# Three PSUM banks for the expert units and three for the attention, instead of two and four

## The chip, the cores and the metric

The kernel runs on one core of one Trainium2 chip. The metric is the device time of one execution in microseconds (us); lower is better. The core has five engines with a queue of instructions each: TensorE (PE, matrix products, with PEld for its weight loads), VectorE (DVE), ScalarE (ACT), GpSimd (POOL) and SyncE (SP, which only issues transfers). Products of TensorE land in PSUM, a small memory of eight banks; here a bank holds 128 partitions by 512 float32 numbers. VectorE and ScalarE read the banks.

## The reference

Causal attention by blocks of 64 over 8 batches, 8 heads, 576 positions and a head size of 64, whose result, put back as 4608 rows of 512, goes through one gated layer with 2048 hidden features:

```python
scores = scale * np.matmul(q, k.transpose(0, 1, 3, 2))
scores = np.where(block_i >= block_j, scores, -1e9)
scores = scores - np.max(scores, axis=-1, keepdims=True)
attn = np.exp(scores)
attn = attn / (np.sum(attn, axis=-1, keepdims=True) + 1e-09)
x = np.matmul(attn, v)          # -> 4608 x 512
h = x @ w_in                    # 512 -> 2048
sp = np.maximum(h, 0.0) + np.log1p(np.exp(-np.abs(h)))
g = h * erf(sp)
return g @ w_out                # 2048 -> 512
```

## The kernel before

**The layer is cut into 144 units.** A unit is 256 rows of `x` by 256 hidden features: 18 blocks of rows times 8 blocks of features. `moe_unit` (L173) makes one. Its *up* part is 24 products of 256 columns (L185: two halves of the features, four slices of the 512 inputs, three terms, since `x` and the weights are kept as pairs of float16 numbers, a high and a low part) and fills one PSUM bank, `h`. `gate` (L145) then computes the gating function from that bank: ScalarE at L154 to L156, VectorE at L157 to L160, ScalarE again at L161 for the high part `gh`, and GpSimd at L162 for the low part `gl`. The bank `h` is read twice, by the first instruction (L154) and by the last of VectorE's (L160), so it is held from the first of the 24 products until L160 has ended. The *down* part is 12 products of 512 columns (L194) from `gh` and `gl` into two banks `o`, which collect over several units. Down parts run three units behind the up parts (`LAG = 3`, L221).

**The attention is cut into 64 heads.** For a head, `maxes` (L387) computes the scores once in five pieces (L394), whose row maxima VectorE takes (L397), and turns the maxima around (L424, ScalarE's copy L426, a transfer at L427). `probs` (L431) computes the scores a second time, transposed, in six pieces of two products each (L440, L441), of which ScalarE takes the exponentials (L445). `pv` (L464) multiplies them with `v` for two heads at a time (L489) and sums them (L512); ScalarE empties both (L492, L514, L515). `normalise` (L541) divides (L550, L551, L564, L569, VectorE's L571) and writes the rows of `x` to memory. Every piece of all this takes one PSUM bank from `bank` (L304), which the named reader empties.

**The eight banks.** `ps_o` has two (for `o`), `ps_h` two (for `h`) and `ps_a` four (for the attention). `bank` takes from `ps_a`, except in the first part of the run, before any rows of `x` are ready (`loaded` is empty): there the units need no bank yet, and of eight calls one goes to `ps_o` and two to `ps_h` (one bank of `ps_o` is held there by products that only keep TensorE busy, L645). When the attention is through, `ps_a` is closed and `ps_h2` takes two of its banks (L695); from there on units take turns between `ps_h` and `ps_h2` (L177).

**The order.** The loop at L648 goes over the heads and merges, at each, the steps of `maxes` two heads ahead, of `probs` for this head, of `pv` and `normalise` for earlier ones, of the weights' conversion (heads 1 to 22: L115 to L121, L141, L142) and of the units (`moe1`, L262: 12 steps at each of the first 20 heads, then 28; a unit is 12 steps). That order is a priority. The framework's scheduler puts the instructions of each engine into their final order when the program is built: it goes by the priority and by when operands and banks come free in its own estimate of the times. A tile gets its bank there as well. On the chip every engine works through its queue in that fixed order, and an instruction whose bank has not been emptied by its former reader holds up everything behind it on its engine.

So the run has four parts: the start, in which only attention runs (its first unit begins at 164.9 us); a part in which units, attention and the conversion of the weights run together; a long middle with units and attention; and an end with units alone.

Of the kernel before, what the change touches and what calls it, by code (L numbers as in the profile page):

```python
# [17 lines left out]
PSUM = bass.MemoryType.PSUM  # L18
# [14 lines left out]
def tile_attention_moe(ctx: ExitStack, tc: tile.TileContext, qk, v, w, maskrows, sels, out):  # L33
# [23 lines left out]
    xpool = ctx.enter_context(tc.tile_pool(name="xpool", bufs=2))  # L57
    mpool = ctx.enter_context(tc.tile_pool(name="mpool", bufs=3))
    ps_o = ctx.enter_context(tc.tile_pool(name="ps_o", bufs=2, space=PSUM))
    ps_h = ctx.enter_context(tc.tile_pool(name="ps_h", bufs=2, space=PSUM))  # L60

    ident = cpool.tile([P, P], F32, name="ident")
    make_identity(nc, ident)
# [59 lines left out]
    def scale_w(g, bank):  # L123

        rs = cpool.tile([P, 2], F32, name=f"wrs{g}")
        nc.vector.tensor_reduce(out=rs, in_=wss[g], axis=AX.X, op=ALU.add)
        pt = bank(f"wt{g}")
        nc.tensor.matmul(pt[:, :2], lhsT=ones, rhs=rs, start=True, stop=True)
        e = cpool.tile([P, 2], F32, name=f"we{g}")
        nc.vector.tensor_copy(e, pt[:, :2])  # L130
        nc.vector.tensor_scalar(out=i32(e), in0=i32(e), scalar1=23, scalar2=None, op0=ALU.logical_shift_right)
        nc.vector.tensor_scalar(out=i32(e), in0=i32(e), scalar1=131, scalar2=None, op0=ALU.add)
        nc.vector.tensor_scalar(out=i32(e), in0=i32(e), scalar1=1, scalar2=None, op0=ALU.logical_shift_right)
        powers(wsb[g][:, 0:2], wsb[g][:, 2:4], e, 15)
# [152 lines left out]
            todo.pop(0)()  # L287

    with tc.tile_pool(name="apool", bufs=2) as apool, tc.tile_pool(name="spool", bufs=1) as spool, \
            tc.tile_pool(name="ps_a", bufs=4, space=PSUM) as ps_a:  # L290
        pstage = [spool.tile([P, n], F32, name=f"p32_{i}") for i, n in enumerate(PN)]
        rss = [spool.tile([P, SH], F32, name=f"rs{i}") for i in range(3)]
        mxs = [spool.tile([P, 7], F32, name=f"mx{i}") for i in range(2)]
# [10 lines left out]
        def bank(name):  # L304

            turn.append(0)
            k = len(turn) % 8 if not loaded else 0
            if k in (2, 5):
                return ps_h.tile([P, 512], F32, tag="h", name=name)
            if k in (3,):  # L310
                return ps_o.tile([P, 512], F32, tag="o", name=name)
            return ps_a.tile([P, 512], F32, tag="a", name=name)
# [13 lines left out]
        def scale_v(b, qd, v32, vt):  # L326

            nm = f"{b}_{qd}"
            vm = apool.tile([P, 1], F32, tag="vm", name=f"vm{nm}")
            nc.vector.tensor_reduce(out=vm, in_=v32, axis=AX.XY, op=ALU.max, apply_absolute_value=True)  # L330
            pt = bank(f"vt{nm}")
            nc.tensor.transpose(out=pt[:1, :P], in_=vm, identity=ident)
            if qd == 0:
                nc.vector.tensor_reduce(out=top_v[b], in_=pt[:1, :P], axis=AX.X, op=ALU.max)
                if b < B32:
                    return
            vs = apool.tile([1, 2], F32, tag="vs", name=f"vs{nm}")
            vs_[b, qd] = vs
            e = apool.tile([1, 2], F32, tag="ve", name=f"ve{nm}")
            if qd:  # L340
                nc.vector.tensor_reduce(out=e[:, :1], in_=pt[:1, :P], axis=AX.X, op=ALU.max)
                nc.vector.tensor_tensor(out=e[:, :1], in0=e[:, :1], in1=top_v[b], op=ALU.max)
            nc.vector.tensor_scalar(out=i32(e[:, :1]), in0=i32(e[:, :1] if qd else top_v[b]), scalar1=23, scalar2=None, op0=ALU.logical_shift_right)
            nc.vector.tensor_scalar(out=i32(e[:, :1]), in0=i32(e[:, :1]), scalar1=77, scalar2=197, op0=ALU.max, op1=ALU.min)
            powers(vs[:, 0:1], vs[:, 1:2], e[:, :1], 10)
# [390 lines left out]
```

## Time and profile before

| | us |
|---|---|
| median of three runs | 1290.05 |
| the three runs | 1290.46, 1290.05, 1287.4 |
| the profiled execution | 1288.4 |
| its span, first to last instruction | 1286.6 |
| DVE busy in the span | 895.8 (70%) |
| ACT busy | 780.5 (61%) |
| POOL busy | 523.6 (41%) |
| mean granted clock of TensorE | 0.975 of full speed |

The profile is of one execution; its time stands 1.65 us under the median of the runs. "Busy" is the time in which an engine has an instruction in work. Matrix products overlap, and the ends of their records are modelled, so a TensorE that is always busy is not one at its peak; but time in which it is not busy is lost to it. Where the profile names a releaser ("DVE m_r L160") it is the instruction whose end was the last thing that the waiting one needed, with its line in the code.

### The profile page before, as it was taken

How to read it: one execution, taken by the hardware profiler on the slowest of the kernel's cores; microseconds unless marked ns; L12 is line 12 of the kernel's file. 1: busy time of each engine (PE TensorE's matmuls, PEld its weight loads, DVE VectorE, ACT ScalarE, POOL GpSimd, SP SyncE). 2: the span in 40 equal slices, each digit the busy share in tenths (PEclk: the TensorE clock that was granted, in tenths of full speed). 3: DMA queues.
4: the chain of work that ended last, by engine and by line, in shares of the span. 5: the costliest groups of instructions: out<-in, count | busy, mean ns of one | idle time of the engine just before them, and what ended most of it. 6: DMA issues, size and time to landing. Idle time of an engine off the chain costs nothing.

```text
span 1286.6 us, 23640 instructions
## 1 busy us (share of the span) xinstructions
PE 1200.5 (93%) x9108; PEld 810.2 (63%) x9108; DVE 895.8 (70%) x1583; ACT 780.5 (61%) x1555; POOL 523.6 (41%) x488
## 2 busy tenths in 40 slices
PE   1899999989999999999999999999999999999997
PEld 0455566556666666767667666766667667666664
DVE  3853689887567878688777778795777765555554
ACT  2453567667556666766666756666666775555553
POOL 4444435553435453545445344544445331321221
PEclk9887889989999999999999999999999999999999
DMA  9794566862454554453545444554444221221111
GB/s 250 210 218 97 125 170 172 229 148 67 109 122 121 135 133 110 105 143 114 110 114 124 111 109 128 131 122 100 115 112 113 63 69 52 82 66 50 53 63 50
DMA packets 95808, 151.74 MB, mean 118 GB/s; under 512 B 7804, under 2 KB 44988, under 8 KB 95696
## 3 DMA queue, kind: packets, MB, share of 16 engines
q1 hardware_dynamic: 69840, 93.34, 24.4%
q0 software_dynamic: 25216, 56.73, 21.5%
q8 instruction: 72, 1.18, 0.4%
q14 instruction: 40, 0.33, 0.1%
q10 hardware_dynamic: 640, 0.17, 0.1%
HBM read 121.73 MB, written 28.31 MB: 117 GB/s over the span
## 4 chain that ended last, share of the span: by engine, by line
PE 49%; DVE 26%; ACT 14%; DMA 5%; issue 4%; POOL 1%; SPq 0%; DVEq 0%; POOLq 0%; ACTq 0%
PE m_h L185 14%; PE o L194 14%; DVE m_r L158 5%; DVE m_r L157 5%; PE u L489 4%; DVE m_r L159 4%; DVE m_r L160 3%; PE t L440 3%; ACT m_r L155 3%; ACT m_r L154 3%; PE s L394 3%; ACT m_r L156 3%; PE t L441 3%; DVE mx L397 2%; PE us L512 2%
## 5 line engine op out<-in xcount | busy, mean ns | idle before, releaser
L185 PE MATMUL m_h<-xh,w 128*128 128x256 f16 x2304 | 476.9, 276 | 12.8 <-DVE m_r L160 12.5
L185 PEld LDWEIGHTS <-w 128*128 128x128 f16 x3456 | 326.7, 99 | 146.6 <-issue 24.1
L194 PE MATMUL o<-w,m_gh 128*128 128x512 f16 x1152 | 337.0, 382 | 10.5 <-DVE pt L235 6.4
L162 POOL TENSOR_TENSOR m_gl<-m_r,m_gh 128x512 f16<-128x512 f32 x144 | 174.3, 1211 | 403.6 <-ACT m_gh L161 362.8
L185 PE MATMUL m_h<-xl,w 128*128 128x256 f16 x1152 | 316.6, 275 | 0.0
L397 DVE TENSOR_REDUCE mx<-s 64x1 f32<-64x288 f32 (+4 forms) x384 | 174.8, 470 | 110.8 <-PE s L394 109.8
L157 DVE SCALAR_TENSOR_TENSOR m_r<-m_r 128x512 f32<-128x512 f32 x144 | 115.6, 803 | 171.1 <-ACT m_r L156 168.9
L445 ACT ACTIVATE p<-t 128x288 f32<-128x288 f32 (+4 forms) x384 | 146.0, 385 | 108.7 <-PE t L441 102.7
L194 PE MATMUL o<-w,m_gl 128*128 128x512 f16 x576 | 206.0, 384 | 0.3 <-POOL m_gl L162 0.3
L161 ACT CAST m_gh<-m_r 128x512 f16<-128x512 f32 x144 | 88.8, 617 | 192.0 <-DVE m_r L160 187.9
L440 PE MATMUL t<-qk 69*128 69x288 f32 (+4 forms) x384 | 168.0, 438 | 13.1 <-DMA qk<-mt 7.5
L394 PE MATMUL s<-qk 68*64 68x288 f32 (+3 forms) x384 | 150.9, 424 | 27.4 <-DVE mx L397 14.9
L382 POOL TENSOR_TENSOR qk<-st,qk 64x576 fp32r<-64x576 f32 x64 | 95.9, 1498 | 149.4 <-DMA qk<-qk 136.2
L154 ACT ACTIVATE m_r<-m_h,c,bs 128x512 f32<-128x512 f32 (+3 forms) x192 | 124.1, 666 | 45.1 <-PE m_h L185 43.0
L194 PEld LDWEIGHTS <-m_gh 128*128 128x128 f16 x1152 | 98.5, 98 | 67.2 <-issue 19.7
L158 DVE SCALAR_TENSOR_TENSOR m_r<-m_r,m_r 128x512 f32<-128x512 f32 x144 | 120.6, 837 | 2.8
L441 PE MATMUL t<-qk 128*128 128x288 f32 (+4 forms) x384 | 120.1, 313 | 0.0
L159 DVE SCALAR_TENSOR_TENSOR m_r<-m_r 128x512 f32<-128x512 f32 x144 | 115.7, 803 | 2.9
L383 POOL TENSOR_TENSOR qk<-st,qk 64x576 fp32r<-64x576 f32 x64 | 103.1, 1611 | 30.0 <-DMA qk<-qk 27.1
L457 DVE TENSOR_TENSOR p<-p,p 128x832 f16<-128x832 f32 x80 | 82.6, 1033 | 36.3 <-ACT p L456 36.2
L156 ACT ACTIVATE m_r<-m_r,c 128x512 f32<-128x512 f32 x144 | 103.7, 720 | 2.9 <-ACT m_r L155 0.8
L155 ACT ACTIVATE m_r<-m_r,c 128x512 f32<-128x512 f32 x144 | 103.8, 721 | 1.7
(98 smaller groups left out, 1484.9 us busy)
## 6 DMA issues: line engine op xcount, KB each, us to landing
qk<-qk POOLq DMA_DIRECT2D x64, 432.0 KB, 5.0
st<-qk SPq DMA_DIRECT2D x64, 288.0 KB
qk<-qk POOLq DMA_DIRECT2D x64, 288.0 KB, 5.2
raw<-w SPq DMA_DIRECT2D x32, 512.0 KB
v<-v SPq DMA_DIRECT2D x16, 640.0 KB
x_d<-xs POOLq DMA_DIRECT2D x32, 288.0 KB, 3.5
xh<-x_d SPq DMA_DIRECT2D x36, 256.0 KB
xl<-x_d SPq DMA_DIRECT2D x36, 256.0 KB
```

The lines of the kernel that those rows point to most:

```text
L154: nc.scalar.activation(r0s[:, :, lo:hi], h[:, :, lo:hi], AF.Tanh, bias=const(p1), scale=bss[b][g][:, 0:1])
L157: nc.vector.scalar_tensor_tensor(out=r0, in0=r0, scalar=c3, in1=r0, op0=ALU.add, op1=ALU.mult)
L158: nc.vector.scalar_tensor_tensor(out=r0, in0=r1, scalar=c4, in1=r0, op0=ALU.add, op1=ALU.mult)
L159: nc.vector.scalar_tensor_tensor(out=r0, in0=r0, scalar=c5, in1=r0, op0=ALU.add, op1=ALU.mult)
L162: nc.gpsimd.tensor_tensor(out=gl, in0=r0, in1=gh, op=ALU.subtract)
L185: nc.tensor.matmul(h[:, k, :], lhsT=wf[:, a, sl], rhs=x[:, cc, :], start=cc == 0 and i == 0, stop=cc == NCC - 1 and i == 2)
L194: nc.tensor.matmul(o[c], lhsT=a[:, sl], rhs=wf[:, b_, :], start=u == u0 and k == 0 and not lo and b_ == 2, stop=u == u1 - 1 and k == nu - ...
L394: nc.tensor.matmul(dst[:r, :w_], lhsT=qh[:K, i * P : i * P + r], rhs=kh[:K, k0 : k0 + w_], start=True, stop=True)
L397: nc.vector.tensor_reduce(out=mx[:r, col : col + 1], in_=src, axis=AX.X, op=ALU.max, negate=True)
L440: nc.tensor.matmul(s[:kk, :w_], lhsT=kh[:K, ks], rhs=qh[:K, q0 : q0 + w_], start=True, stop=False)
L441: nc.tensor.matmul(s[:kk, :w_], lhsT=klh[:, ks], rhs=qhl[:, q0 : q0 + w_], start=False, stop=True)
L445: nc.scalar.activation(p32s[part][:kk, c : c + w_ - skip], s[:kk, skip:w_], AF.Exp, scale=SCALE)
```

## The change

`ps_h` gets a third bank and `ps_a` loses its fourth. In the first part of the run, of eight calls of `bank` three now go to `ps_h` instead of two, and four instead of five to `ps_a`. All eight banks stay in use, and no instruction is added or taken away.

```diff
-    ps_h = ctx.enter_context(tc.tile_pool(name="ps_h", bufs=2, space=PSUM))
+    ps_h = ctx.enter_context(tc.tile_pool(name="ps_h", bufs=3, space=PSUM))
...
-            tc.tile_pool(name="ps_a", bufs=4, space=PSUM) as ps_a:
+            tc.tile_pool(name="ps_a", bufs=3, space=PSUM) as ps_a:
...
             k = len(turn) % 8 if not loaded else 0
-            if k in (2, 5):
+            if k in (2, 5, 7):
                 return ps_h.tile([P, 512], F32, tag="h", name=name)
             if k in (3,):
                 return ps_o.tile([P, 512], F32, tag="o", name=name)
             return ps_a.tile([P, 512], F32, tag="a", name=name)
```

## The prediction, made before the changed kernel was run

> **What bounds the kernel now.** I read the page's first two parts, then the busy time in the four parts of the run, then the waits of TensorE in each part, then single stretches of the timeline. The page first: the share of each engine, and in 40 slices the busy tenths of PE and its granted clock.
>
> ```profile
> PE 1200.5 (93%) x9108; PEld 810.2 (63%) x9108; DVE 895.8 (70%) x1583; ACT 780.5 (61%) x1555; POOL 523.6 (41%) x488
> ...
> PE   1899999989999999999999999999999999999997
> ...
> PEclk9887889989999999999999999999999999999999
> ```
>
> PE is the engine that is nearly always at work. By the parts of the run (window, its length, then busy time and count for PE, PEld, DVE, ACT and POOL, granted clock, DMA share, GB/s):
>
> ```profile
> 0.00:165.00 165.00, 125.87 (x692) 68.84 (x693) 92.23 (x203) 69.73 (x174) 72.43 (x90) 0.88 0.75 182
> 165.00:300.00 135.00, 122.42 (x906) 82.51 (x906) 120.04 (x226) 92.00 (x211) 66.20 (x57) 0.94 0.67 170
> 300.00:1075.00 775.00, 756.17 (x6154) 529.74 (x6153) 571.91 (x997) 509.91 (x1000) 338.81 (x302) 1.00 0.45 111
> 1075.00:1287.00 212.00, 196.09 (x1361) 129.14 (x1359) 111.58 (x161) 108.90 (x171) 46.17 (x40) 0.99 0.18 58
> ```
>
> In the middle (300 to 1075 us) PE rests 775.0 - 756.2 = 18.8 us, 2.4%; DVE is busy 74% of it and ACT 66%. There PE's queue sets the time: each us that PE waits less or more comes off or goes onto the run. From 165 to 300 us DVE is busy 120.0 of 135 us, 89%, and PE 122.4: both near the limit. Before 165 us the DMA share is 0.75 and PE rests 39 us; after 1075 us PE rests 16 us.
>
> What does PE wait for? First the `h` banks, whose release is L160. Lines from the views of L160 (who waited for it in the whole run: us, times) and of L185 in the middle (idle of PE and PEld ahead of L185 until L160 ended):
>
> ```profile
>   PE m_h L185: 12.5, 19
>   PEld L185: 7.0, 10
> ...
> L185 PE MATMUL m_h<-xh,w x1560: 269/273/437, 300.2 to 1074.4; 128*128 128x256 f16 x195
> ...
>   DVE m_r L160: 15.6, 22
> ```
>
> A unit has 16 of the products counted here, so 97 units start in the middle, one in 8 us. The whole run has 19.5 us of waits of PE and its weight loads for an `h` bank, 15.6 of them in the middle, in 22 waits of 0.71 us each; the same view of the last part has 3.4 us:
>
> ```profile
>   DVE m_r L160: 3.4, 5
> ```
>
> Then the banks of the attention, whose readers are L397, L445 and others: the two largest such waits of PE from 165 to 300 us, and the largest two of L394 and L440 in the middle.
>
> ```profile
> PE s L394 <- DVE mx L397: 3.2, 2, 2.4
> PE t L440 <- DVE mx L397: 2.6, 2, 1.8
> ...
> PE s L394 <- DVE mx L397: 0.6, 1, 0.6
> PE t L440 <- DVE mx L397: 0.5, 1, 0.5
> ```
>
> With four banks the middle loses about 1 us to them. The profile says: `h` is the short pool, `ps_a` is not. The question is what `ps_a` loses with its fourth bank.
>
> **The change, part by part. (1) The third `h` bank.** One unit start of the kind that waits, on the timeline (start, duration, engine, line; in brackets the idle time and what ended it):
>
> ```profile
> 494.54 0.67 DVE L160 SCALAR_TENSOR_TENSOR m_r<-m_r,m_h 128x512 f32<-128x512 f32 x1
> 495.26 0.55 PEld L185 LDWEIGHTS <-w 128*128 128x128 f16 x6 [0.53 <-DVE m_r L160]
> ```
>
> L160 ends at 495.21 and the unit two later starts at once. With a third bank it needs the bank of the unit before that one, empty a whole unit, 8 us, earlier. No wait in the trace is near 8 us, so all of these can go: **-19.5 us at most**, nothing at least (if PE only meets the next wait). What would be late next is the buffers of `gh` and `gl`, four of each for a lag of three; nobody waits for them now on PE's side. I take -17: the 15.6 of the middle and 1.4 of the 3.9 elsewhere, where other engines are as late. The two pools that units use by turns at the end, three and two banks instead of two and two, bring nothing more: after 1112 us, when both are open, no unit waits for its bank.
>
> **(2) The fourth bank gone, middle.** No view shows this wait, since it isn't there yet. I bound it from the order in which banks are opened (first product into one) and emptied (end of its last reader), each product matched with its reader by the order of the queues: an opening that finds three earlier attention banks unread has to wait, with three banks, until the first of them is read. The worst case of the middle:
>
> ```profile
> 464.91 0.38 PE L394 MATMUL s<-qk 68*64 68x288 f32 x1
> 465.13 0.99 PE L569 MATMUL rb<-ident,rw 128*128 128x128 f32 x5
> 466.30 0.56 PE L440 MATMUL t<-qk 69*128 69x448 f32 x1
> 467.69 1.02 DVE L457 TENSOR_TENSOR p<-p,p 128x832 f16<-128x832 f32 x1
> 469.23 0.44 DVE L397 TENSOR_REDUCE mx<-s 64x1 f32<-64x288 f32 x1
> 469.59 0.92 DVE L571 SCALAR_TENSOR_TENSOR usb<-usb,ratio,rb 128x384 f32<-128x384 f32 x2
> ```
>
> L394 opens one bank, L569 two. DVE is busy with the gate and L457 and reads them only at 469.23 and 469.59. The product of 466.30 would wait until L397 ends at 469.67: 3.37 us. Behind it in PE's queue stand the up and down products of the units and, on ACT, the exponential L445 of that piece. Of some 650 openings in the middle 58 find three banks unread, the first and the last of them these:
>
> ```profile
> 314.02 0.27 PE L424 MATMUL mt<-ident,mx 128*5 128x128 f32 x1
> ...
> 1030.29 0.36 PE L440 MATMUL t<-qk 69*64 69x256 f32 x1
> ```
>
> Their waits add to 37.7 us. Openings less than 3 us apart share one cause, which makes 40 groups; the longest wait of each adds to 31.2 us. So the bounds are 0, if the scheduler sees each shortage and puts a unit's products first, and **+37.7**. The scheduler does see some: a unit holds its `h` bank for some 15 us (by the same matching) and one starts every 8 us, so two banks are nearly always full, and yet only 22 of 97 unit starts wait. But it goes by its own times, and what it leaves is 0.71 us a wait, from the row of 15.6 us. I take 25 waits of the 40 groups at 0.71 us: **+18**.
>
> **(3) The same from 165 to 300 us.** 38 openings find three banks unread (first and last below), with waits of 22.6 us in all and 13.0 us by groups, 12 of them.
>
> ```profile
> 170.84 0.38 PE L354 MATMUL vb<-vs,ones 1*128 1x2 f32 x2
> ...
> 282.29 0.30 PE L394 MATMUL s<-qk 68*64 68x288 f32 x1
> ```
>
> Here even four banks run out (the 3.2 and 2.6 us above). But PE rests 12.6 us already, and a DVE that is busy 89% is what the banks wait for; a wait of PE costs only where it later leaves DVE without work. Bounds 0 and +22.6; I take half of the grouped sum, **+7**.
>
> **(4) The clock.** A stall can cost more than its length. The clock of two neighbouring stretches, and the row in PE's timeline inside the second:
>
> ```profile
> 870.00:880.00 10.00, 9.98 (x88) 7.31 (x86) 5.45 (x10) 7.53 (x15) 2.36 (x3) 1.00 0.47 129
> 880.00:890.00 10.00, 9.23 (x56) 6.38 (x54) 5.14 (x11) 4.55 (x10) 3.95 (x3) 0.83 0.43 81
> ...
> 881.79 1.47 PE L550 MATMUL rt<-sel,rs 128*128 128x4 f32 x12 [0.77 <-DVE mx L397]
> ```
>
> A rest of 0.77 us ahead of products of only four columns, and the clock falls to 0.83 over 10 us: 0.17 x 10 = 1.7 us lost. It is the only such fall in the middle. I count one more, **+2**, with bounds 0 and +5 (three).
>
> The Trainium skill ("TensorE: Matmul & The Clock Gate", "Why this matters for your kernels") warns only of rests of PE over some 3 us, which bring half the clock back. By that rule just the one wait of 3.37 us would cost a fall. The trace differs, since a rest of 0.77 us stands ahead of one here; the measurement decides, and it speaks a little more against the change.
>
> **(5) The start.** Up to 165 us a bank of `ps_a` comes round after five to seven calls of `bank`, before (four banks for calls 0, 1, 4, 6, 7 of eight) as after (three for 0, 1, 4, 6); one of `ps_h` after eight in both. The longest waits there are for a transfer and for DVE, which has not begun:
>
> ```profile
> PE s L394 <- DMA qk<-maskrows: 11.9, 2, 6.3
> PE s L394 <- DVE mx L397: 11.1, 2, 10.6
> ```
>
> Their cover, the DMA, stays: 0, within 3 us either way.
>
> **The sum.** -17 + 18 + 7 + 2 + 0 = +10, on the profiled execution of 1288.4 us (1286.6 span and 1.8 around it): 1298.4. The median of the runs stands 1.65 us higher, so **1300.0 us**, 0.8% slower.
>
> **The rivals.** *Faster: the waits for `h` go and `ps_a` doesn't miss its bank.* Mechanism: in the middle the scheduler fills each shortage of an attention bank with a unit's products, which a third `h` bank makes ready earlier. For it: PE's waits on `h` are 60% of its rest in the middle (11.2 of 18.8 us on PE itself, row below), and only 58 of 650 openings need the fourth bank. Against it: the late readers are late by the chip's times. It decides where (2), (3) and (4) together stay under 17 us. Price: -17 and some 2 left of the rest, 1273.4, or about 1275 beside the median.
>
> ```profile
> PE m_h L185 <- DVE m_r L160: 11.2, 16, 1.6
> ```
>
> The Trainium skill has this rule ("Perfetto Trace Analysis", "Optimization Strategy"): the same bubble again and again on the engine that should be saturated can mean that there is no memory for the next tile. It points at `h`, and the trace agrees that this bubble repeats; the rule says nothing on the pool that pays.
>
> *No change.* Gain and cost meet: (2) to (4) cost 13 to 21 us. 1286 to 1294.
>
> *Much slower.* Nothing is foreseen, every wait is paid: -17 + 37.7 + 22.6 + 5 = +48, 1338.
>
> *The third bank isn't used*, because units come up in the queue only after the old bank is free: +27 without the -17, 1317. Against it are the 22 starts in the middle that stand waiting.
>
> **How the numbers follow.** Forecast (slower, 1294 to 1325, the third bank unused among it): 0.5. Faster rival: 0.25. No change: 0.2. Much slower: 0.05. About 0.3%, 3.9 us here, is what a measurement of this kernel can tell from no change: faster means under 1286.2, slower over 1293.9. Range: 1274 to 1325; it takes in the faster case nearly whole and leaves out the much slower one and the tail under 1274. The forecast's own range is 1294 to 1325.
>
> **What would show it.** In the changed kernel's profile: the waits for L160 ahead of L185 near 0 in the whole run (step 1); new waits of PE at L394, L440, L424, L550 and L569 for L397, L445, L571, 15 to 25 us in the middle (step 2) and more than 5.8 us for L397 before 300 us (step 3); one or two more slices of the clock under 1.0 (step 4); the first unit still near 165 us (step 5). It is wrong if the waits on L160 stay, or if PE's rest in the middle falls under 10 us.

## The result, and the profile after

| | before | changed |
|---|---|---|
| median of 20 runs, us | 1290.9 | 1301.55 |
| lowest to highest, us | 1280.92 to 1302.79 | 1290.27 to 1311.61 |
| the profiled execution, us | 1288.4 | 1290.27 |

The ratio is 1.0083 with a 95% interval of [1.0059, 1.0107]: slower by 0.8%. The profiled execution of the changed kernel was the quickest of its 20 runs. A second profile, taken in experiment 2, was of the slowest of its own six runs (1312.62 us, lowest 1299.3), so the two stand on both sides of the median. The profiled execution of the last experiment was a disturbed one of 5600.53 us, and no time in it is used.

First the page of the changed kernel, the lines that answer to those of before:

```profile
PE 1191.3 (92%) x9108; PEld 800.9 (62%) x9108; DVE 901.0 (70%) x1583; ACT 781.1 (61%) x1555; POOL 526.7 (41%) x488
...
PE   1899898989989999999999999999999999999997
...
PEclk9999899989999999999999999999999999999999
```

The span is only 2 us longer, but the clock in the first eighth is not that of before (99998 against 98878). The parts have to be compared by the work in them. I take the middle from the first product of the first unit of row block 3 to that of block 14, the same work in each kernel: 300 to 1066 us before, 287 to 1068 us in the first profile of the changed kernel, 305 to 1090 us in the second (columns as in the prediction: length, then busy time and count of PE, PEld, DVE, ACT, POOL).

```profile
300.00:1066.00 766.00, 747.17 (x6085) 523.60 (x6084) 567.66 (x990) 503.64 (x990) 336.49 (x300) 1.00 0.45 112
```

```profile
287.00:1068.00 781.00, 752.71 (x6088) 522.88 (x6087) 575.32 (x1002) 507.22 (x995) 337.05 (x300) 1.00 0.44 111
```

```profile
305.00:1090.00 785.00, 754.44 (x6086) 524.82 (x6085) 577.18 (x1002) 506.59 (x994) 336.30 (x300) 0.99 0.45 110
```

The same 6086 or so products take 15 and 19 us more, and PE rests 28.3 and 30.6 us instead of 18.8. The view of L160, whole run, shows that nobody on PE waits for a unit's bank any more; only ACT is left in the list:

```profile
who waited for it (us, times):
  ACT m_gh L161: 183.5, 109
```

And the waits of PE in the middle, first profile (us in total, times, longest):

```profile
PE t L440 <- DVE mx L397: 8.5, 7, 2.0
PE u L489 <- DVE p L457: 7.0, 8, 1.4
PE mt L424 <- DVE mx L397: 3.1, 3, 1.6
PE us L512 <- DVE mx L397: 2.3, 2, 2.0
PE s L394 <- DVE mx L397: 1.7, 2, 1.5
PE us L512 <- ACT p L445: 1.6, 2, 1.1
PE t L440 <- ACT p L445: 1.5, 3, 0.7
```

All but the second line are first products into a bank that wait for the reader of another tile: L440 does not use what L397 makes, it needs the bank that L397 empties. With the smaller ones they make 21 us in 26 waits, from about 2 us. (The second line waits for data.)

The start differs for another reason. First unit's products in the changed kernel, first and second profile (first and last start, within the first 300 us), and the clock in the stretch up to it:

```profile
L185 PE MATMUL m_h<-xh,w x216: 269/273/437, 149.9 to 299.0; 128*128 128x256 f16 x108
...
0.00:150.00 150.00, 111.56 (x686) 61.85 (x687) 97.79 (x202) 69.14 (x174) 74.53 (x89) 0.98 0.83 202
```

```profile
L185 PE MATMUL m_h<-xh,w x184: 269/273/437, 165.7 to 298.9; 128*128 128x256 f16 x184
...
0.00:165.00 165.00, 122.83 (x684) 66.76 (x684) 94.05 (x200) 69.28 (x172) 72.72 (x88) 0.89 0.78 183
```

One kernel, two executions, 16 us apart: with the clock at 0.98 the first unit begins at 149.9 us, at 0.89 at 165.7 us (before: 164.9 us at 0.88). So the first profile's early start is its clock, not the change, and it hid nearly all of the loss of the middle.

Over whole runs the clock counts in the same way. In 64 runs of the kernel before, timed beside the experiments (one of 1985.02 us left out), a straight line through span and mean granted clock falls by some 11 us for each 0.01 of clock. Where two kernels are compared below and their clocks differ, this line gives an estimate of what the clock did.

Idle time isn't all of a wait, because a product's record is longer than the time after which the next can start (270 ns for 256 columns, one every 109 ns). For the middle I therefore also added, over all first products into a bank, by how much the step from the product before exceeds the usual step (lower quartile of the same pair of products in the kernel before), leaving out the stretches of half clock, whose excess stands in the last column:

| kernel (banks: units + attention) | middle, us | at units' banks | at attention's banks | half clock |
|---|---|---|---|---|
| before (2 + 4) | 765.9 | 13.8 | 9.2 | 1.7 |
| changed (3 + 3), first profile | 780.7 | 0.1 | 36.4 | 3.4 |
| changed, second profile | 785.0 | 0.1 | 37.5 | 6.7 |
| one bank unused (2 + 3) | 779.0 | 8.8 | 30.3 | 1.7 |
| (4 + 2) | 799.2 | 0.3 | 54.2 | 6.5 |

From before to changed: -13.7 at the units' banks, +27.2 at the attention's, +1.7 of clock: together +15.2, for the +14.8 us of the middle.

### The profile page after: what moved, and what is told of

Read it like the earlier page. It is cut to its first block, busy times and chain, and to the rows that moved or that the text cites. A ratio compares the mean times of both kernels' runs of the same rounds, so it can differ in the third digit from the quotient of the medians.

```text
span 1288.5 us, 23626 instructions
## 1 busy us (share of the span) xinstructions
PE 1191.3 (92%) x9108; PEld 800.9 (62%) x9108; DVE 901.0 (70%) x1583; ACT 781.1 (61%) x1555; POOL 526.7 (41%) x488
## 4 chain that ended last, share of the span: by engine, by line
PE 43%; DVE 27%; ACT 15%; DMA 7%; issue 5%; POOL 2%; SPq 0%; DVEq 0%; POOLq 0%; ACTq 0%
PE m_h L185 13%; PE o L194 13%; DVE m_r L158 5%; DVE m_r L157 5%; DVE m_r L159 4%; PE u L489 4%; DVE m_r L160 4%; ACT m_r L155 3%; ACT m_r L156 3%; DMA raw<-w 3%; ACT m_r L154 3%; PE t L440 3%; PE s L394 2%; DVE mx L397 2%; PE t L441 2%
## 5 line engine op out<-in xcount | busy, mean ns | idle before, releaser
L397 DVE TENSOR_REDUCE mx<-s 64x1 f32<-64x288 f32 (+4 forms) x384 | 174.9, 471 | 109.7 <-PE s L394 108.5
L157 DVE SCALAR_TENSOR_TENSOR m_r<-m_r 128x512 f32<-128x512 f32 x144 | 119.2, 828 | 166.1 <-ACT m_r L156 165.8
L440 PE MATMUL t<-qk 69*128 69x288 f32 (+4 forms) x384 | 164.0, 428 | 22.0 <-DVE mx L397 11.7
L394 PE MATMUL s<-qk 68*128 68x256 f32 (+3 forms) x384 | 148.5, 419 | 25.3 <-DVE mx L397 13.5
L382 POOL TENSOR_TENSOR qk<-st,qk 64x576 fp32r<-64x576 f32 x64 | 98.6, 1540 | 164.6 <-DMA qk<-qk 151.0
L158 DVE SCALAR_TENSOR_TENSOR m_r<-m_r,m_r 128x512 f32<-128x512 f32 x144 | 120.4, 836 | 2.8
L159 DVE SCALAR_TENSOR_TENSOR m_r<-m_r 128x512 f32<-128x512 f32 x144 | 117.8, 818 | 2.9
L383 POOL TENSOR_TENSOR qk<-st,qk 64x576 fp32r<-64x576 f32 x64 | 100.7, 1573 | 27.1 <-DMA qk<-qk 24.2
L440 PEld LDWEIGHTS t<-qk 69*128 69x128 f32 (+1 forms) x384 | 70.0, 182 | 58.9 <-DVE mx L397 17.7
L156 ACT ACTIVATE m_r<-m_r,c 128x512 f32<-128x512 f32 x144 | 103.7, 720 | 2.8 <-ACT m_r L155 0.7
L457 DVE TENSOR_TENSOR p<-p,p 128x832 f16<-128x832 f32 x80 | 82.0, 1025 | 32.8 <-ACT p L456 32.6
```

Of the source, the lines that this page charges most:

```text
L157: nc.vector.scalar_tensor_tensor(out=r0, in0=r0, scalar=c3, in1=r0, op0=ALU.add, op1=ALU.mult)
L158: nc.vector.scalar_tensor_tensor(out=r0, in0=r1, scalar=c4, in1=r0, op0=ALU.add, op1=ALU.mult)
L159: nc.vector.scalar_tensor_tensor(out=r0, in0=r0, scalar=c5, in1=r0, op0=ALU.add, op1=ALU.mult)
L394: nc.tensor.matmul(dst[:r, :w_], lhsT=qh[:K, i * P : i * P + r], rhs=kh[:K, k0 : k0 + w_], start=True, stop=True)
L397: nc.vector.tensor_reduce(out=mx[:r, col : col + 1], in_=src, axis=AX.X, op=ALU.max, negate=True)
L440: nc.tensor.matmul(s[:kk, :w_], lhsT=kh[:K, ks], rhs=qh[:K, q0 : q0 + w_], start=True, stop=False)
```

## The experiments

Each run was timed in five rounds beside the kernel before on the same chip. The theory at the outset was the prediction's: the units gain some 17 us, the attention pays more.

**1. The fourth bank taken away and given to nobody.**

```diff
-            tc.tile_pool(name="ps_a", bufs=4, space=PSUM) as ps_a:
+            tc.tile_pool(name="ps_a", bufs=3, space=PSUM) as ps_a:
```

> ps_a with three banks, ps_h still with two: one bank stays unused, and the start is as before. Theory (a trade: the units gain some 17 us, the attention pays some 27): the waits on L160 ahead of L185 stay near 19.5 us, the attention's bank waits of PE in the middle come to 15 to 25 us as in the changed kernel, and the time is 15 to 30 us over the kernel before (1306 to 1320). Rival (the fourth bank of the attention isn't missed, and the changed kernel is slower through a worse order of the queues): within 5 us of the kernel before.

Measured: 1306.56 us against 1290.86, ratio 1.0143 [1.0089, 1.0197]. Waits of PE in the middle:

```profile
304.00:1083.00 779.00, 751.52 (x6087) 522.12 (x6085) 572.40 (x989) 504.96 (x990) 338.97 (x300) 1.00 0.44 110
...
PE t L440 <- DVE mx L397: 8.6, 8, 2.0
PE m_h L185 <- DVE m_r L160: 6.8, 10, 1.4
```

The theory holds in kind: the lost bank alone makes the kernel slower, by 15.7 us at the median. But the waits on L160 did not stay at 19.5 us; they fell to 14.2 (8.7 on PE and 5.5 on its weight loads), as they would if a PE that waits at the attention's banks reaches the units' later. By the table the third unit bank then takes 8.7 us more off, and 6.1 us of it come back at the attention's banks, where PE now arrives earlier. The step from this kernel to the changed one is worth -17 us in no view: the middle is no shorter with the third unit bank (779.0 us without it, 780.7 and 785.0 with it), and the medians say -3.55, within their spread.

**2. The changed kernel once more**, for the second profile used above.

> The changed kernel again, for a second profile: the first had a start 15 us shorter than before's, with its clock at 0.98 instead of 0.88 there. If that came from the clock of the one execution, this profile can have a first unit near 165 us again, and the middle is 12 to 20 us longer than before's in both. If the change itself shortens the start, the first unit begins near 150 us again. Time 1296 to 1306.

Measured: 1303.01 us, ratio 1.011 [1.006, 1.016]. First unit at 165.7 us, middle 19 us longer: the first reading.

**3. One pool of six banks.** `ps_a` and `ps_h2` are left out, `bank` and the units take from `ps_h` alone (but for the call in eight that goes to `ps_o` at the start).

```diff
-    ps_h = ctx.enter_context(tc.tile_pool(name="ps_h", bufs=2, space=PSUM))
+    ps_h = ctx.enter_context(tc.tile_pool(name="ps_h", bufs=6, space=PSUM))
...
-            if k in (2, 5):
-                return ps_h.tile([P, 512], F32, tag="h", name=name)
...
-            return ps_a.tile([P, 512], F32, tag="a", name=name)
+            return ps_h.tile([P, 512], F32, tag="h", name=name)
```

> One pool of six banks for the units and the attention together, in the whole run. Theory (each side has spare banks when the other is short): no waits on L160 over 5 us, waits on attention banks in the middle under 10 us, and a time under the kernel before, 1272 to 1288. Rival (a unit holds a bank for some 15 us, so units take the banks and the attention runs on fewer): 1295 to 1320, with waits on attention banks over 20 us in the middle.

Measured: 1298.44 us, ratio 1.0069 [1.0038, 1.01]; slower, against the theory. From 156 to 306 us PE waits for the units' rows of `x` (us in total, times, longest):

```profile
PE m_h L185 <- DMA xh<-x_d: 20.7, 2, 11.7
```

With so many banks free the units come up in PE's queue before their rows of `x` have been loaded. (The changed kernel has one such wait, 4.9 us.) Not all of it is lost: block 3 begins at 306 us, 6 us later than before. In the middle the steps at banks come to 1.2 us for the units and 18.9 for the attention, 2.9 us less than before, and the idle waits stay within the theory's limits (0.6 us on L160, some 10 at the attention's banks). The time went against it all the same: half-clock stretches cost 9.8 us in the middle, and the mean granted clock of its runs is 0.974, where the kernel before has 0.979 beside it. By the line above that is some 5 of the 7.6 us, an estimate.

**4. Further the same way, four and two.**

```diff
-    ps_h = ctx.enter_context(tc.tile_pool(name="ps_h", bufs=2, space=PSUM))
+    ps_h = ctx.enter_context(tc.tile_pool(name="ps_h", bufs=4, space=PSUM))
...
-            tc.tile_pool(name="ps_a", bufs=4, space=PSUM) as ps_a:
+            tc.tile_pool(name="ps_a", bufs=2, space=PSUM) as ps_a:
...
-            if k in (2, 5):
+            if k in (2, 5, 6, 7):
```

> One step further the same way: four banks for the units, two for the attention. Theory: nothing more to gain on the units' side, where no wait on L160 is left with three; the attention's waits grow much, 40 to 100 us over the kernel before. Rival (the scheduler's order hides the shortage): under 20 us over it.

Measured: 1327.44 us, ratio 1.0296 [1.0251, 1.0341], 36.6 us over the kernel before, a little under the range that the theory gave. The middle's steps at the attention's banks grow to 54.2 us; the units had nothing left to gain.

**5 and 6. VectorE's queue made shorter, in both kernels.** Why are the readers late? One of the gate's four operations is left out.

```diff
-        nc.vector.scalar_tensor_tensor(out=r0, in0=r1, scalar=c4, in1=r0, op0=ALU.add, op1=ALU.mult)
```

> The kernel before without L158, one of the four operations of VectorE in the gate (the gating function lacks one factor): 144 x 0.84 = 120 us less for VectorE. It is the partner of the next run. Both theories: somewhat faster than the kernel before, by 5 to 25 us, since the units' banks are emptied 0.84 us earlier.

> The changed kernel, also without L158. Theory (a wait on an attention bank is VectorE being late, with the gate's block of operations and L457 in front of the reader): with VectorE's queue shorter the attention's first products lose less, and the difference to the previous run falls from some 11 us to under 5, the waits of PE on attention banks in the middle from some 21 us to under 12. Rival (three banks are too few for the number of pieces in flight, whoever is late): the difference stays at 9 us or more.

Measured: 1264.53 us with two and four banks, 1264.75 us with three and three (ratios to the kernel before 0.9817 [0.9769, 0.9866] and 0.9807 [0.9751, 0.9863]). The first is 26 us under its kernel before, just over the range given, and by the time the difference between the two is gone. In the middle of the second one (lines stand one higher up: L439 is L440), then of the first:

```profile
285.00:1038.00 753.00, 744.97 (x6086) 522.19 (x6085) 494.87 (x901) 509.29 (x994) 330.29 (x301) 1.00 0.47 114
...
PE us L511 <- ACT p L444: 1.7, 1, 1.7
PE t L439 <- DVE mx L396: 1.5, 3, 0.8
```

```profile
302.00:1049.00 747.00, 741.11 (x6085) 522.56 (x6085) 491.73 (x894) 508.17 (x992) 331.41 (x301) 1.00 0.47 115
...
PE m_h L184 <- DVE m_r L159: 0.4, 1, 0.4
```

With DVE busy 66% of the middle instead of 74%, waits on attention banks fall from 21 to 4 us with three banks, and waits on the units' banks from 11.2 to 0.4 us with two. Neither pool is far short when VectorE is in time. But the equal times are in part the clock's: the six runs with three and three have a mean granted clock of 0.987, the other six 0.979, and by the line above some 8 us would be left at an equal clock, an estimate. The middles, with the clock at 1.00 in both, are still 6 us apart (753 and 747 us, 15 to 19 without this edit). So the theory has the waits right, and most of the middle's loss; that the difference falls under 5 us is not shown by this pair. Experiments 11 and 12 make a pair of equal clocks.

**7. The start's share of the banks as it was, with three and three.**

```diff
-            if k in (2, 5, 7):
+            if k in (2, 5):
```

> The changed kernel with the start's share of the banks as it was (two of eight calls to the units' pool instead of three, the other five to the attention's three banks). Expected by the prediction: within 4 us of the changed kernel (1298 to 1307). Rival (the third edit is what keeps the start from losing): 6 us or more over it.

Measured: 1296.84 us (12 runs), ratio 1.0075 [1.0035, 1.0115]; the interval holds the changed kernel's 1.0083. The median lies just under the range expected. The third edit makes no difference that these runs tell.

**8. The pool of six, units later.**

```diff
-        PRIO = {}
+        PRIO = {"moe": 100}
```

> The pool of six for all, and the units' steps put 100 places later in the scheduler's priority (about one unit). The pool of six lost 20.7 us where units came up in the queue before their rows had been loaded, and only some 20 us to banks in the middle. Theory: later units don't meet that wait, it falls under 5 us, and the time is 1280 to 1290, under the kernel before. Rival (the early wait only fills a time in which PE has nothing to do, and the order of the middle gets worse): 1293 or more.

Measured: 1331.32 us, ratio 1.0354 [1.0308, 1.04]. The theory failed: the wait for the rows is still 13.8 us, and the middle takes 810 us instead of 775 with the pool of six as it was. The order that the priority gives matters more than the wait that it was to remove; why the middle grew so much wasn't followed up.

**9 and 10. VectorE relieved without leaving anything out.** L457 goes to GpSimd.

```diff
-                nc.vector.tensor_tensor(out=pl, in0=p32s[part], in1=ph, op=ALU.subtract)
+                nc.gpsimd.tensor_tensor(out=pl, in0=p32s[part], in1=ph, op=ALU.subtract)
```

> The kernel before with L457 (the low part of the probabilities, 80 operations, 82.6 us of VectorE) given to GpSimd, and nothing left out. Theory (what a bank waits for is VectorE being late): VectorE is 814 us busy instead of 896, the waits on L160 in the middle fall from 15.6 to under 6 us, and the time is 5 to 20 us under the kernel before (1271 to 1286). Rival (GpSimd takes 1.2 us for 512 columns, so some 2 us a piece and 160 us in all, and L489 waits for it instead): within 5 us of it or slower, with waits of L489 on L457 over 15 us instead of 4.3.

> The changed kernel with the same edit. Theory: the waits of PE on attention banks in the middle fall from 21 us to under 14, and the difference to the previous run is under that of 11 us between the changed kernel and the one before, 0 to 8 us. Rival (the shortage does not hang on VectorE's load): 9 us or more over the previous run.

Measured: 1336.21 us, ratio 1.0344 [1.0284, 1.0404], and 1349.85 us, 1.0459 [1.0399, 1.052]. The theory fell: the kernel with two and four is 43 us slower, not faster. The rival had the direction and the wait for GpSimd at L489 (17.1 us), not the size. VectorE's busy time fell by 13 us only, to 882.5, though 82.6 us of work had left it. Groups of that kernel and its wait on GpSimd (busy us, mean ns, idle before):

```profile
L157 DVE SCALAR_TENSOR_TENSOR m_r<-m_r 128x512 f32<-128x512 f32 x144 | 146.4, 1016 | 226.8 <-ACT m_r L156 223.2 <-POOL m_gl L162 3.1
L457 POOL TENSOR_TENSOR p<-p,p 128x832 f16<-128x832 f32 x80 | 142.1, 1776 | 97.5 <-ACT p L456 89.0 <-PE s L394 3.3 <-PE o L194 2.8
L489 PE MATMUL u<-p,v 128*64 128x320 f16 (+9 forms) x1176 | 95.6, 300 | 17.1 <-POOL p L457 17.1
```

L157, untouched, takes 1016 ns in the mean instead of 803. The waits of PE on L160 rose to 26.1 us with two unit banks. With three and three the waits at the attention's banks in the middle rose as well, from 21 to some 29 us, and the two kernels stand 13.6 us apart: this run's rival had the number, but the question it put stays open here, since VectorE was not relieved. GpSimd's work makes VectorE late.

**11 and 12. GpSimd's work taken away instead.** L382 and L383 are left out; a set of zeros at the start stands in for one of the low parts.

```diff
+        for q_ in qks:
+            nc.gpsimd.memset(f32(q_[:D, :S]), 0.0)
...
-                nc.gpsimd.tensor_tensor(out=t[:D, 0, :], in0=st[:D, :], in1=f32(t[:D, 2, :]), op=ALU.subtract)
-                nc.gpsimd.tensor_tensor(out=t[D:, 1, :], in0=st[D:, :], in1=f32(t[D:, 1, :]), op=ALU.subtract)
```

> The kernel before without L382 and L383, GpSimd's 128 operations of 1.5 to 1.6 us that make the low parts of q and k (one term of the scores is zero, the other keeps the unsplit value). In the trace of before, those of L157 to L159 that run while a GpSimd operation runs take 0.8 to 2.7 us instead of 0.69, 55 us in all, 40 of them beside L382 and L383. Theory (VectorE is late because those stand in its way): VectorE 30 to 50 us less busy, waits on L160 in the middle under 8 us instead of 15.6, time 8 to 25 us under the kernel before. Rival (its lateness comes from the length of its queue): VectorE hardly less busy, waits and time within 5 us of before.

> The changed kernel with the same left out. Theory: the waits of PE on attention banks in the middle fall from 21 us to under 12 and the difference to the previous run to under 6 us. Rival: waits over 16 us and a difference of 8 us or more.

Measured: 1277.54 us with two and four, 1277.22 us with three and three, ratios 0.9912 [0.9881, 0.9944] and 0.9915 [0.9884, 0.9947]: faster, and no difference between the splits, at mean granted clocks of 0.979 and 0.980. VectorE runs the same 1583 instructions in 838.1 us instead of 895.8. In the first of the two:

```profile
L157 DVE SCALAR_TENSOR_TENSOR m_r<-m_r 128x512 f32<-128x512 f32 x144 | 106.6, 740 | 175.5 <-ACT m_r L156 174.5
L158 DVE SCALAR_TENSOR_TENSOR m_r<-m_r,m_r 128x512 f32<-128x512 f32 x144 | 103.8, 721 | 2.9
L159 DVE SCALAR_TENSOR_TENSOR m_r<-m_r 128x512 f32<-128x512 f32 x144 | 99.9, 694 | 2.9
...
311.00:1058.00 747.00, 741.02 (x6082) 522.25 (x6081) 531.63 (x989) 507.70 (x989) 210.81 (x219) 1.00 0.41 100
...
PE m_h L185 <- DVE m_r L160: 1.7, 4, 0.8
```

PE rests 6.0 us in the middle, 18.8 before. The second kernel's waits are not known, since its profile is the disturbed one. The leaving out also frees GpSimd's queue and makes a head's operands ready sooner, so not all of the gain need come from VectorE; that wasn't separated.

## Why the prediction came out, point by point

The time, 1300.0 against 1301.55, is right, and so are the direction and the mechanism: the waits left the units' banks and came back, larger, at the attention's. That the time came so close is partly luck. Taking the fourth bank away alone cost 15.7 us, where steps 2 to 4 have 27; adding the third unit bank after it brought 3.55 us, where step 1 has 17. The two errors nearly cancel.

- **Step 1, the third bank: right in the waits, too large as time.** The waits on L160 are gone to the last one. By the steps between products that is 13.7 us in the middle, for 15.6 predicted. The 1.4 us taken elsewhere can't be seen: the last part, from the first product of block 14 on, has 220.5 us before and 220.8 and 220.7 in the two profiles. The experiment with a bank unused shows what the prediction did not reckon with: the two terms are not independent. Some of what PE saves at one pool it loses by coming earlier to the other, so the third bank was worth 3.55 us by the medians, not 17.
- **Step 2, the fourth bank: mis-sized.** +18 was predicted; idle time says 21 us, the steps between products +27. The guess of 25 waits at 0.71 us was close for idle time (26 waits of 0.80 us); as time it was too small, and the 31.2 us of the grouped bound was nearer. What it left out: a wait costs more than the idle time that a trace of overlapping products shows.
- **Step 3, 165 to 300 us: too large.** From the first unit to block 3 the kernels take 135.3 us before, 137.2 and 139.4 after: +2 to +4 for +7. A new wait stands there that no step named, 4.9 us of PE for rows of `x` not yet loaded.
- **Step 4, the clock: right in size.** The middle has 1.7 us of half clock before, 3.4 and 6.7 after: +1.7 and +5.0 for +2.
- **Step 5, the start: no effect shown.** First unit at 164.9 us before, 149.9 and 165.7 after, by the clock of the execution.

Steps 2 and 3 erred in opposite directions. The middle's +15 and +19 are more than the +10.65 of the medians. Single executions differ by over 20 us, and the one profiled before was a quick one for its clock: the line through the 64 runs gives 1292.7 us at its clock of 0.975, and its span was 1286.6. That may be what the middles show too much; no second profile of the kernel before settles it.

The faster rival named the right reason why it might fail (the readers are late by the chip's times) without knowing what makes them so. The rule of the Trainium skill on repeated bubbles ("Perfetto Trace Analysis", "Optimization Strategy") found the short pool, and the bubble went away; time went the other way, since the bank came from a pool whose readers were the same late engine.

## What to carry to other kernels

Before a bank is moved from one pool to another, count in the trace how often the giving pool has its last bank in use, and for how long; a pool without waits is not a pool with a spare bank. If both pools are emptied by the same engine, and that engine is late, moving banks only moves the wait: with part of GpSimd's work taken away, both splits took the same time (1277.54 and 1277.22 us). And compare stretches of equal work rather than spans when the clock of a start can differ by 16 us between two executions of one kernel.

## What the runs showed of the hardware

The gate's VectorE operations with both inputs in SBUF (L157 to L159) get longer when an operation of GpSimd is running as they start; L160, with one input in PSUM, doesn't. In the kernel before (minimum, median and longest in ns, same size and number):

```profile
L157 DVE SCALAR_TENSOR_TENSOR m_r<-m_r x144: 627/693/2712, 170.2 to 1275.8; 128x512 f32<-128x512 f32 x144
...
L160 DVE SCALAR_TENSOR_TENSOR m_r<-m_r,m_h x144: 622/686/690, 174.8 to 1278.1; 128x512 f32<-128x512 f32 x144
```

L157 reads `r0` twice, from SBUF; L160 reads `r0` and the bank. L157 took up to 2712 ns; L160 never took over 690, though 21 of its 144 began while an operation of GpSimd still had 0.7 to 1.3 us to run. The means of L157, L158 and L159 (803, 837 and 803 ns against some 690) make 54 us of VectorE's 896, in pieces of up to 2 us; without L382 and L383 12 us are left (740, 721, 694). The Trainium skill ("SBUF — State Buffer", "SBUF: two separate sides") says that VectorE and GpSimd share a pair of ports, which one of them holds for its whole instruction while the other stands still, for VectorE's operations with two inputs in SBUF among others. The traces agree. Of L157 to L159, 65 took more than 750 ns; each of them began while a GpSimd instruction was running, and 63 ended 0.55 to 0.56 us after it, however early they had begun. One of them, behind L382 (start, duration, in us):

```profile
368.80 1.40 POOL L382 TENSOR_TENSOR qk<-st,qk 64x576 fp32r<-64x576 f32 x1 [1.68 <-DMA qk<-qk]
368.93 1.81 DVE L157 SCALAR_TENSOR_TENSOR m_r<-m_r 128x512 f32<-128x512 f32 x1
```

So what VectorE loses is the rest of the GpSimd operation, up to all of it, not a share. None of the 43 in whose course a GpSimd instruction began, with none running at their start, took over 693 ns.
